# Decode attention with two layers of cached K and V: packets of wo, the place where p is turned, and the size of the chain's bursts

## The chip, the cores and the metric

The kernel runs on one core of one Trainium2 chip. The metric is the device time of one execution in microseconds. Ten runs of the kernel before have a median of 1128.28 us (1122.96 to 1136.9).

## What is computed

Eight batch elements, one token each (D = 448), pass twice through the same two blocks. Block A is attention over a cache: 16 query heads of 256, 8 K/V heads, 4096 cached positions. Block B is a small mixer and MLP. With one token the mixer's shifted parts are all zero, so that `hs` is zero and `x1 = x`. The core of the reference:

```python
def A(x, k_cache, v_cache, wq, wo):          # k_cache, v_cache: (8, 8, 4096, 256)
    q = (x @ wq).reshape(B, 1, 16, 256).transpose(0, 2, 1, 3)
    k, v = repeat(k_cache, 2, axis=1), repeat(v_cache, 2, axis=1)
    p = softmax(einsum("bhqd,bhkd->bhqk", q, k) * 256 ** -0.5)
    o = einsum("bhqk,bhkd->bhqd", p, v)
    return o.transpose(0, 2, 1, 3).reshape(B, 1, 4096) @ wo

x = x + A(layernorm(x), k_cache, v_cache, wq, wo)
x = x + B(layernorm(x), w1, w2, w3, w4)      # ends in x1 + gelu(layernorm(x1) @ w3) @ w4
x = x + A(layernorm(x), k_cache, v_cache, wq, wo)
x = x + B(layernorm(x), w1, w2, w3, w4)
```

K and V of one element and one pass are 32 MB in bfloat16. Both passes read the same caches, and the second pass of an element can start only when the first has gone through the whole of both blocks.

## The kernel before

**Slots and items.** SBUF has 15 slots of 1 MB, [128, 4096] bfloat16. A task is (pass, element, pair of K/V heads). It has 8 items: four slots of K and four of V. `items` (lines 534 to 542) holds their order, in which the K items of one task alternate with the V items of the task before: K, V, K, V. Each item works on one slot, then the slot's place goes back to `places` (line 804), and `emit_loads` (line 559) issues the next load into it from SyncE (line 576). The order of the loads is that of the items.

**What stays.** Of each element, the eleven slots in `kept` (line 63) stay in SBUF from pass 0 to pass 1, and a twelfth is held in four PSUM banks (`away`, line 609, and `back`, line 616). While the eleven are held, four slots are left to circulate.

**A K item.** `transpose_k` (line 579): two VectorE transposes of 32x32 blocks in place (L584, 1219 ns each). Then `step`, then `scores` (line 586): 32 products (L592) in two halves of 16; the second half reads what the second transpose wrote. After the second and the fourth K item of a task, `exps` (line 600) lets ScalarE write p. After the first K item of the next task, `transpose_p` (line 623) turns p with four products against an identity (L628), and ScalarE copies the result into `ptw` (L635). Kept K's are not transposed again in pass 1.

**A V item.** `step`, then `pv` (line 640): 16 products of `ptw` with the slot (L647). In the last eight V items of the program `pv_cols` (line 656) takes the slot as weights instead (L661), in columns of d.

**The chain of an element.** When half of an element's head pairs are done in pass 0, `first_half` (line 452) is added, and when all are, `chain` (line 461): the sums of exp (`z_cols`, line 395), the turn of o to columns (`half`, line 426, L443), products with wo (`add_cols`, line 328, L339), the norm (line 198), w3 (`mlp_hidden`, line 350, L357), w4 (`out_cols`, line 321, L339), and the projection of q for pass 1 (`project_q`, line 277, L285). They are generators. Each `yield` ends a burst. `first_last`, `last` and `rest` are the same for pass 1; `rest` does blocks A's end and B for the first four elements together.

**The order.** It is written out in the program's own order on every engine. `step(idx)` (line 696) is called twice per item, before its products (lines 743, 761) and at its end (line 806). It lets each kind of generator go to its next `yield` when it is behind its pace:

```python
if e["n"] < e["of"] * (idx - e["at"] + 1) / max(e["until"] - e["at"], 1):
```

`of` is the number of bursts that `add_gen` is told, `at` and `until` the items between which they are to be spread. So at most two bursts of a kind fall on one item. `spread_q` (line 297, L305 and L311) places the new q for the scores before the first K item of a new element and pass; a chain that is not through by then is run to its end there (lines 726 and 727).

**Where d lies.** `half` turns o in two products (line 443), of d 0 to 127 and of d 128 to 255, so `OT[:, j, h]` holds d = 128 j + partition of head h. wo is loaded with row g x 128 + partition in `wo_sb[partition, g]` (line 678), and `OT[:, i % 2, i // 2]` is multiplied with `wo_sb[:, i]`.

Of the kernel before, what the change touches and what calls it, by code (L numbers as in the profile page):

```python
# [17 lines left out]
def kernel(  # L18
# [27 lines left out]
    nc = tc.nc  # L46
# [3 lines left out]
    Dh = A_k_cache.shape[3]  # L50
# [6 lines left out]
    NB2 = HD // 128  # L57
    HC = F // 128
# [218 lines left out]
    def project_q(b0, nb, qT):  # L277

        yield from norm(xT[:, :, b0 : b0 + nb], nb, False)
        q_ps = room_ps("q", nb).rearrange("p (c b) -> p c b", b=nb)  # L280
        for j in range(2):
            for h in range(Hq):
                for fc in range(4):
                    w, xi = wblk(wq_sb, HD, 2 * h + j, fc)
                    nc.tensor.matmul(  # L285
                        q_ps[:, j * Hq + h, :],
                        w,
                        xbs(nb)[:, xi, :],
                        start=(fc == 0),
                        stop=(fc == 3),  # L290
                    )
                if h % 8 == 7:
                    yield
        nc.vector.tensor_copy(qT, q_ps)
        yield
# [21 lines left out]
    def y_room(nb):  # L317

        return room_ps("y", nb).rearrange("p (u f b) -> p u f b", u=2, b=nb)

    def out_cols(rhs, w, n, b0, nb, every):

        y_ps = y_room(nb)[:, 0]
        yield from add_cols(y_ps, rhs, w, range(n), every)
        xs = xT[:, :, b0 : b0 + nb]
        nc.vector.tensor_add(xs, xs, y_ps)
# [23 lines left out]
    def mlp_hidden(b0, nb):  # L350

        yield from norm(xT[:, :, b0 : b0 + nb], nb, True)
        h_ps = room_ps("h", nb)
        for c in range(HC):
            for fc in range(4):
                w, xi = wblk(w3_sb, F, c, fc)
                nc.tensor.matmul(  # L357
                    h_ps[:, c * nb : c * nb + nb],
                    w,
                    xbs(nb)[:, xi, :],  # L360
                    start=(fc == 0),
                    stop=(fc == 3),
                )
            if c == HC // 2:
                yield
        yield
        g_t = chn.tile([128, 2, HC * MID], FP32, tag="g")
        hh, g0 = g_t[:, 0, 0 : HC * nb], g_t[:, 1, 0 : HC * nb]
        if nb == 1:
            HT_t = chn.tile([128, HC, 1], BF16, tag="HT")  # L370
            HT = HT_t[:]
        else:
            HT = HTw[:, :, b0 : b0 + nb]

        nc.vector.tensor_scalar_mul(hh, h_ps, 0.5)  # L375
        nc.vector.scalar_tensor_tensor(g0, hh, 2 * 0.044715, h_ps, ALU.mult, ALU.mult)
        nc.vector.scalar_tensor_tensor(g0, g0, 1.0, h_ps, ALU.add, ALU.mult)
        nc.scalar.activation(g0, g0, ACT.Tanh, scale=0.7978845608028654)  # L378
        yield
        nc.vector.scalar_tensor_tensor(  # L380
            HT,
            g0.rearrange("p (c b) -> p c b", b=nb),
            1.0,
            hh.rearrange("p (c b) -> p c b", b=nb),
            ALU.add,
            ALU.mult,
        )
        yield
        return HT

    def mlp(b0, nb):
        HT = yield from mlp_hidden(b0, nb)
        yield from out_cols(lambda c: HT[:, c, :], w4_sb, HC, b0, nb, 2)

    def z_cols(zall, gps):

# [29 lines left out]
    def half(o_ps, zall, g8, OT):  # L426


        rz = yield from z_cols(zall, range(2 * g8, 2 * g8 + 2))

        R = chn.tile([128, 8], FP32, tag="R")
        nc.vector.tensor_mul(
            R[:].rearrange("p (g n) -> p g n", n=4),
            rz[:].rearrange("p n g -> p g n"),
            fold[:].rearrange("p (g n) -> p g n", n=4),
        )
        o_sb = chn.tile([128, Dh], FP32, tag="o_sb")
        nc.scalar.copy(o_sb[:], o_ps[:, 0:Dh])  # L438
        in_use.remove(o_ps)
        yield  # L440
        ot_ps = ot_bank[:, 32 * g8 : 32 * g8 + 16].rearrange("p (j h) -> p j h", j=2)
        for j in range(2):
            nc.tensor.matmul(  # L443
                ot_ps[:, j], o_sb[:, 128 * j : 128 * j + 128], R[:], start=True, stop=True
            )
        yield
        nc.vector.tensor_copy(OT[:, :, 8 * g8 : 8 * g8 + 8], ot_ps)
        yield
# [3 lines left out]
    def first_half(b, st):  # L452

        OT = work.tile([128, 2, Hq, 1], BF16, tag="OT", bufs=1)
        st["OT"] = OT
        yield from half(st["o", 0], st["z"], 0, OT[:, :, :, 0])
        yield from add_cols(
            y_room(1)[:, 0], lambda i: OT[:, i % 2, i // 2], wo_sb, range(NB2 // 2), 2
        )

    def chain(b, st):
        OT = st["OT"]
        yield from half(st["o", 1], st["z"], 1, OT[:, :, :, 0])
        yield from add_cols(
            y_room(1)[:, 1], lambda i: OT[:, i % 2, i // 2], wo_sb, range(NB2 // 2, NB2), 2
        )
        xs = xT[:, :, b : b + 1]
        nc.vector.tensor_add(xs, xs, y_room(1)[:, 0])
        nc.vector.tensor_add(xs, xs, y_room(1)[:, 1])
        yield from mlp(b, 1)  # L470
        qT = chn.tile([128, NB2], BF16, tag="qT2", bufs=2)
        yield from project_q(b, 1, qT[:].unsqueeze(2))
        state[1, b] = {"qT": qT}
# [21 lines left out]
    def rest():  # L495

        yield from out_cols(lambda i: OT2[:, i % 2, i // 2, :MID], wo_sb, NB2, 0, MID, 1)
        yield from mlp(0, MID)
        nc.vector.memset(HTw[:, :, 0:MID], 0.0)
        yield  # L500
# [82 lines left out]
            w = t[:].bitcast(U32).rearrange("p (y e w) -> p y e w", e=2, w=64)[:, :, half]  # L583
            nc.vector.transpose(w, w)  # L584

    def scores(t, x, qbd, gp):
        kv = t[:].rearrange("p (k t e i r) -> p k e r t i", k=4, t=4, e=4, r=2)
        for n in range(8):
            half, e2, par = n // 4, (n // 2) % 2, n % 2
            ep = 4 * e2 + 2 * par + half  # L590
            for k in range(4):
                nc.tensor.matmul(  # L592
                    sc[32 * k : 32 * k + 8, 128 * x : 128 * x + 128],
                    qbd[:, ep, gp].rearrange("p a h -> p (a h)"),
                    kv[:, k, 2 * half + e2, par],
                    start=(n == 0),
                    stop=(n == 7),
                )
# [57 lines left out]
    def pv_cols(o_ps, v, a, gp):  # L656

        g = 2 * gp + a // 2
        for y in range(16):
            for j in range(2):  # L660
                nc.tensor.matmul(  # L661
                    o_ps[:, j, 2 * g : 2 * g + 2],
                    v[:, y * Dh + 128 * j : y * Dh + 128 * j + 128],
                    ptw[:, a, 4 * (y % 4) + y // 4, 6:8],
                    start=(a % 2 == 0 and y == 0 and j == 0),
                    stop=(a % 2 == 1 and y == 15),
                    skip_group_check=True,
                )
# [6 lines left out]
    ps0 = rows_to_cols(x_row, Bn)  # L675
    nc.vector.tensor_copy(xT[:], ps0)
    emit_loads(5)
    nc.sync.dma_start(wo_sb[:], A_wo.rearrange("(g p) d -> p g d", p=128))
    load_split(w3_sb, B_w3, F)
    nc.sync.dma_start(w4_sb[:], B_w4.rearrange("(c p) d -> p c d", p=128))  # L680
    for _ in project_q(0, Bn, qT1[:]):
# [11 lines left out]
    def add_gen(kind, b, g, at, until, total):  # L693
        gens.append({"kind": kind, "b": b, "g": g, "at": at, "until": until, "n": 0, "of": total})

    def step(idx):

        for kind in ("chain", "last", "rest"):
# [5 lines left out]
            if e["n"] < e["of"] * (idx - e["at"] + 1) / max(e["until"] - e["at"], 1):  # L704
                e["n"] += 1
                if next(e["g"], gens) is gens:
                    gens.remove(e)

    first_of = {}
    for idx, (n, kv, c) in enumerate(items):  # L710
        first_of.setdefault((tasks[n][:2], kv), idx)
# [2 lines left out]
    for idx, it in enumerate(items):  # L714
        n, kv, c = it
        ps, b, gp = tasks[n]
        if (ps, b, gp, kv, c) == (0, Bn - 1, REST, 0, 0):
            assert pairs_done[1, MID - 1] == 4
            add_gen("rest", 0, rest(), idx + 1, idx + 18, 21)
        p = where[(b, gp), (kv, c)] if ps == 1 and (stays(it) or inside(it)) else where[it]  # L720
        slot = slots[p]
        final = (ps, b) == (1, Bn - 1)
        if kv == 0:
# [17 lines left out]
            if not (ps == 1 and stays(it)):  # L741
                transpose_k(slot)
            step(idx)
            scores(slot, c, st["q"], gp)
            if c == 0 and n - 1 in p_of:
                transpose_p(p_of.pop(n - 1))
            if c == 1:
                p_n = work.tile([128, 4, 32, 4], BF16, tag="p_sb", bufs=1)
                p_of[n] = p_n
# [5 lines left out]
        else:  # L755
# [34 lines left out]
            if c == 3:  # L790
                done = pairs_done[ps, b] = pairs_done.get((ps, b), 0) + 1
                if done == 2 and ps == 0:
                    add_gen("chain", b, first_half(b, st), idx + 1, idx + 21, 9)
                elif done == 2:
                    add_gen("chain" if final else "last", b, first_last(b, st), idx + 1, idx + 13, 9)
                elif done == 4 and ps == 0:
                    add_gen("chain", b, chain(b, st), idx + 1, first_of[(1, b), 0] - 1, 30)
                elif done == 4 and not final:
                    add_gen("last", b, last(b, st), idx + 1, idx + (7 if b == Bn - 2 else 13), 6)
        if not (ps == 0 and stays(it)):  # L800
# [78 lines left out]
```

The softmax here doesn't subtract the row's maximum and nothing guards it: scores larger than these inputs give would overflow.

## Time and profile before

| | |
|---|---|
| Median of ten runs | 1128.28 us |
| Profiled execution | 1129.44 us, its span 1127.6 us |
| TensorE matmul busy | 713.9 us, 63% of the span |
| TensorE weight load busy | 523.8 us, 46% |
| VectorE busy | 590.9 us, 52% |
| ScalarE busy | 124.3 us, 11% |
| GpSimd busy | 15.7 us, 1% |
| Mean granted TensorE clock | 0.611 |
| Read from HBM | 446.77 MB, 396 GB/s over the span |
| Loads of 1 MB slots | 416 (200 K, 216 V), on SyncE's queue |
| Load of wo | one, 3584 KB, issued at 11.42 us |

How to read what follows. The page of a profile has the busy time of each engine, and the span cut into 40 slices of 28.19 us; for each slice it gives the busy share in tenths, and for the DMA engines the GB/s that they moved. In a timeline a line has the start in us, the time that a group of like instructions took, engine and line of the code, operation, what it writes and reads with the shapes, and the number of instructions; in brackets stands the idle time of the engine before it and what ended it. PE is TensorE's products, PEld its weight loads, DVE is VectorE, ACT ScalarE, SPq SyncE's queue of DMA issues. In a list of waits a line has who waited for whom: us in total, times, longest. Matmuls are pipelined and their ends are modelled, so the busy time of TensorE says less than when a group begins.

### The profile page before, as it was taken

How to read it: one execution, taken by the hardware profiler on the slowest of the kernel's cores; microseconds unless marked ns; L12 is line 12 of the kernel's file. 1: busy time of each engine (PE TensorE's matmuls, PEld its weight loads, DVE VectorE, ACT ScalarE, POOL GpSimd, SP SyncE). 2: the span in 40 equal slices, each digit the busy share in tenths (PEclk: the TensorE clock that was granted, in tenths of full speed). 3: DMA queues.
4: the chain of work that ended last, by engine and by line, in shares of the span. 5: the costliest groups of instructions: out<-in, count | busy, mean ns of one | idle time of the engine just before them, and what ended most of it. 6: DMA issues, size and time to landing. Idle time of an engine off the chain costs nothing. (4 is left out here: it accounts for less than half of the span.)

```text
span 1127.6 us, 36977 instructions
## 1 busy us (share of the span) xinstructions
PE 713.9 (63%) x17173; PEld 523.8 (46%) x17173; DVE 590.9 (52%) x1009; ACT 124.3 (11%) x362; POOL 15.7 (1%) x25
## 2 busy tenths in 40 slices
PE   3145677656864577546785477845777476867676
PEld 2123455434642455424564255623565355655555
DVE  5145454646365555546366463655537553575462
ACT  0001001110110011100011001101011001111010
POOL 0000000000000000000000000000000000000000
PEclk9999999655565555655555555555555555565565
DMA  9999999999999999999999999999999999999994
GB/s 353 371 420 420 413 376 408 418 416 391 402 419 421 386 390 417 418 421 391 374 421 419 420 392 400 421 419 417 403 401 419 416 397 392 419 370 398 391 418 177
DMA packets 67242, 449.15 MB, mean 398 GB/s; under 512 B 6921, under 2 KB 12945, under 8 KB 13457
## 3 DMA queue, kind: packets, MB, share of 16 engines
q1 hardware_dynamic: 67056, 446.80, 97.9%
q8 instruction: 134, 2.20, 0.8%
q14 instruction: 20, 0.16, 0.0%
q10 hardware_dynamic: 32, 0.00, 0.0%
HBM read 446.77 MB, written 0.01 MB: 396 GB/s over the span
## 5 line engine op out<-in xcount | busy, mean ns | idle before, releaser
L584 DVE STREAM_TRANSPOSE slot<-slot 128x1024 uint32<-128x1024 uint32 x400 | 469.5, 1219 | 270.8 <-DMA slot<-in_A_k_cache_dram 263.9
L592 PE MATMUL sc<-slot,qbd 128*8 128x128 bf16 x8192 | 280.6, 295 | 291.9 <-DVE slot L584 239.4
L592 PEld LDWEIGHTS <-qbd 128*8 128x8 bf16 x8192 | 198.4, 109 | 369.8 <-issue 189.1
L647 PE MATMUL o<-slot,ptw 128*8 128x256 bf16 x3968 | 250.5, 400 | 60.4 <-DMA slot<-in_A_v_cache_dram 40.6
L601 ACT ACTIVATE p_n<-sc 128x256 bf16<-128x256 f32 x128 | 95.7, 748 | 767.4 <-PE sc L592 767.4
L647 PEld LDWEIGHTS <-ptw 128*8 128x8 bf16 x3968 | 111.8, 112 | 108.0 <-issue 55.8
L339 PEld LDWEIGHTS <-wo_sb 128*128 128x128 bf16 (+1 forms) x1600 | 63.6, 123 | 21.4 <-issue 21.0
L339 PE MATMUL misc<-OT,wo_sb 128*128 128x1 bf16 (+1 forms) x1280 | 54.3, 176 | 7.2 <-issue 5.0
L285 PEld LDWEIGHTS <-wq_sb 128*128 128x128 bf16 x1152 | 34.9, 104 | 25.2 <-issue 19.5
L311 DVE TENSOR_SCALAR qbd<-misc,quad 128x64 bf16<-128x64 f32 x64 | 13.8, 278 | 60.0 <-PE misc L305 60.0
L635 ACT CAST ptw<-misc 128x128 bf16<-128x128 f32 x64 | 17.4, 272 | 201.6 <-PE misc L628 111.1
L285 PE MATMUL misc<-xb,wq_sb 128*128 128x1 bf16 x1024 | 32.3, 165 | 8.6 <-DVE xb L260 4.4
L601 ACT ACTIVATION_READ_ACCUMULATOR p_n<-sc 128x1 f32 x128 | 33.9, 265 | 0.0
L443 PEld LDWEIGHTS misc<-R,o_sb 128*128 128x128 f32 x124 | 28.0, 314 | 10.4 <-issue 8.2
L443 PE MATMUL misc<-R,o_sb 128*128 128x8 f32 x124 | 30.8, 359 | 1.1 <-ACT o_sb L438 1.1
L243 POOL TENSOR_TENSOR t<-t,nhalf 128x2 f32<-128x2 f32 (+2 forms) x18 | 13.3, 740 | 1098.3 <-DVE t L250 1098.3
L339 PEld LDWEIGHTS <-w_sb 128*128 128x128 bf16 (+1 forms) x630 | 25.0, 125 | 6.0 <-issue 5.8
L357 PE MATMUL misc<-xb,w_sb 128*128 128x1 bf16 (+1 forms) x560 | 17.9, 165 | 12.4 <-DVE xb L260 7.4
L357 PEld LDWEIGHTS <-w_sb 128*128 128x128 bf16 x560 | 17.7, 105 | 17.0 <-issue 16.9
L412 PE MATMUL misc<-zm,one 128*128 128x8 f32 (+1 forms) x66 | 18.8, 355 | 9.4 <-ACT ptw L635 6.5
L619 DVE STREAM_TRANSPOSE slot<-store 128x512 uint32<-128x512 uint32 x32 | 20.1, 685 | 7.2 <-PE sc L592 7.2
L415 DVE RECIPROCAL rz<-misc 128x8 f32<-128x8 f32 (+1 forms) x33 | 6.3, 192 | 32.4 <-PE misc L412 30.6
(94 smaller groups left out, 256.6 us busy)
## 6 DMA issues: line engine op xcount, KB each, us to landing
slot<-in_A_v_cache_dram SPq DMA_DIRECT2D x216, 1024.0 KB, 11.6
slot<-in_A_k_cache_dram SPq DMA_DIRECT2D x200, 1024.0 KB, 12.3
wo_sb<-in_A_wo_dram SPq DMA_DIRECT2D x1, 3584.0 KB, 26.7
wq_sb<-in_A_wq_dram SPq DMA_DIRECT2D x3, 1024.0 KB, 6.9
w_sb<-in_B_w_dram SPq DMA_DIRECT2D x1, 1568.0 KB, 12.7
w_sb<-in_B_w_dram SPq DMA_DIRECT2D x3, 448.0 KB, 26.6
wq_sb<-in_A_wq_dram SPq DMA_DIRECT2D x2, 256.0 KB, 10.1
w_sb<-in_B_w_dram SPq DMA_DIRECT2D x2, 112.0 KB
```

The source lines that it names most:

```text
L285: nc.tensor.matmul(q_ps[:, j * Hq + h, :], w, xbs(nb)[:, xi, :], start=(fc == 0), stop=(fc == 3),)
L311: nc.vector.tensor_scalar_mul(qbd[:, :, :, a, :], qs.rearrange("p e (f g u h) -> p (e f) u g h", f=2, u=2, h=2)[:, :, u], quad[:, a : a + 1],)
L339: nc.tensor.matmul(r, w[:, i, lo:hi], rhs(i), start=start, stop=stop, skip_group_check=open is not None,)
L357: nc.tensor.matmul(h_ps[:, c * nb : c * nb + nb], w, xbs(nb)[:, xi, :], start=(fc == 0), stop=(fc == 3),)
L412: nc.tensor.matmul(z_ps, ones, zm[:], start=True, stop=True)
L443: nc.tensor.matmul(ot_ps[:, j], o_sb[:, 128 * j : 128 * j + 128], R[:], start=True, stop=True)
L584: nc.vector.transpose(w, w)
L592: nc.tensor.matmul(sc[32 * k : 32 * k + 8, 128 * x : 128 * x + 128], qbd[:, ep, gp].rearrange("p a h -> p (a h)"), kv[:, k, 2 * half + e2, ...
L601: nc.scalar.activation(p_sb[:, :, :, 2 * u : 2 * u + 2].rearrange("p t i x -> p x t i"), sc[:, 256 * u : 256 * u + 256].rearrange("p (x t ...
L619: nc.vector.transpose(slot[:].bitcast(U32)[:, 512 * n : 512 * n + 512], store[n][:].bitcast(U32))
L635: nc.scalar.copy(ptw[:, :, :, 6:8], pt_ps.rearrange("p t k (a h) -> p a (t k) h", a=4),)
L647: nc.tensor.matmul(o_ps[32 * q : 32 * q + 8, 0:256], ptz[:, at : at + 8], v[:, y * Dh : (y + 1) * Dh], start=(begin and y < 4), stop=(y >= ...
```

## The change

Three edits, and what follows from them.

1. **wo.** Row (h x 256 + 2 x partition + j) of wo now goes to `wo_sb[partition, 2 h + j]`. Two neighbouring rows of 896 bytes go to one partition, as one run of 1792 bytes. So that OT fits, `half` takes every second column of `o_sb` as weights, and `pv_cols` every second column of the V slot: `OT[:, j, h]` holds d = 2 x partition + j.
2. **p.** `transpose_p` is called inside `scores` of the first K item of the next task, between the 16th and the 17th product, instead of after the 32nd.
3. **Bursts.** `project_q` yields after every 4 heads (16 products) instead of 8, `mlp_hidden` after every 4 columns blocks (16 products) instead of twice in all, and the products with wo in pass 0 and with w4 after every block of columns (16 and 14) instead of every two. The numbers of bursts told to `add_gen` are raised to match: 9 to 11, 30 to 40, 21 to 25.

The products, their number, the transposes and the loads of K and V are the same, and so is the order of the loads on SyncE's queue.

```diff
@@ project_q
-                if h % 8 == 7:
+                if h % 4 == 3:
                     yield
@@ mlp_hidden
-            if c == HC // 2:
+            if c % 4 == 3:
                 yield
@@ mlp
-        yield from out_cols(lambda c: HT[:, c, :], w4_sb, HC, b0, nb, 2)
+        yield from out_cols(lambda c: HT[:, c, :], w4_sb, HC, b0, nb, 1)
@@ half
-                ot_ps[:, j], o_sb[:, 128 * j : 128 * j + 128], R[:], start=True, stop=True
+                ot_ps[:, j], o_sb[:].rearrange("p (i j) -> p j i", j=2)[:, j], R[:], start=True, stop=True
@@ first_half
-            y_room(1)[:, 0], lambda i: OT[:, i % 2, i // 2], wo_sb, range(NB2 // 2), 2
+            y_room(1)[:, 0], lambda i: OT[:, i % 2, i // 2], wo_sb, range(NB2 // 2), 1
@@ chain
-            y_room(1)[:, 1], lambda i: OT[:, i % 2, i // 2], wo_sb, range(NB2 // 2, NB2), 2
+            y_room(1)[:, 1], lambda i: OT[:, i % 2, i // 2], wo_sb, range(NB2 // 2, NB2), 1
@@ scores
-    def scores(t, x, qbd, gp):
+    def scores(t, x, qbd, gp, between=None):
         kv = t[:].rearrange("p (k t e i r) -> p k e r t i", k=4, t=4, e=4, r=2)
         for n in range(8):
             half, e2, par = n // 4, (n // 2) % 2, n % 2
+            if n == 4 and between is not None:
+                between()
@@ pv_cols
-                    v[:, y * Dh + 128 * j : y * Dh + 128 * j + 128],
+                    v[:, y * Dh + j : (y + 1) * Dh : 2],
@@ the loads at the start
-    nc.sync.dma_start(wo_sb[:], A_wo.rearrange("(g p) d -> p g d", p=128))
+    nc.sync.dma_start(
+        wo_sb[:].rearrange("p (h j) d -> p h (j d)", j=2),
+        A_wo.rearrange("(h p j) d -> p h (j d)", p=128, j=2),
+    )
@@ the loop over the items
+    def TURN(n):
+        return 0
...
-            add_gen("rest", 0, rest(), idx + 1, idx + 18, 21)
+            add_gen("rest", 0, rest(), idx + 1, idx + 18, 25)
...
-            scores(slot, c, st["q"], gp)
-            if c == 0 and n - 1 in p_of:
-                transpose_p(p_of.pop(n - 1))
+            turn = None
+            if c == TURN(n) and n - 1 in p_of:
+                turn = lambda t=p_of.pop(n - 1): transpose_p(t)
+            scores(slot, c, st["q"], gp, between=turn)
...
-                    add_gen("chain", b, first_half(b, st), idx + 1, idx + 21, 9)
+                    add_gen("chain", b, first_half(b, st), idx + 1, idx + 21, 11)
...
-                    add_gen("chain", b, chain(b, st), idx + 1, first_of[(1, b), 0] - 1, 30)
+                    add_gen("chain", b, chain(b, st), idx + 1, first_of[(1, b), 0] - 1, 40)
```

## The prediction

> **What bounds the kernel now.** I read the page's slices and queues first: how full are the DMA engines, and where not?
>
> ```profile
> DMA  9999999999999999999999999999999999999994
> GB/s 353 371 420 420 413 376 408 418 416 391 402 419 421 386 390 417 418 421 391 374 421 419 420 392 400 421 419 417 403 401 419 416 397 392 419 370 398 391 418 177
> q1 hardware_dynamic: 67056, 446.80, 97.9%
> ```
>
> The DMA engines are busy all the time, but the busy share hides the loss; the GB/s line shows it. Undisturbed slices move 421 GB/s, so one 1 MB slot takes 1.0486/421 = 2.49 us. Adding (421 - r)/421 x 28.19 us over slices 3 to 39 gives 36.4 us lost, 32.3 of it in the sixteen slices at 403 or below. Those come in eight groups, one for each batch element.
>
> Next, what the load queue waits for: SyncE's own waits.
>
> ```profile
> SPq L576 <- PE o L647: 204.7, 134, 7.3
> SPq L576 <- DVE slot L584: 184.2, 63, 5.0
> SPq L576 <- PE sc L592: 105.7, 117, 3.3
> ```
>
> A load is issued when PV (L647) or scores (L592) has read its slot. Where eight loads are queued this costs nothing. The stretches (view by windows: PE, PEld, DVE, ACT, POOL busy with counts, clock, DMA share, GB/s) tell full from thin:
>
> ```profile
> 38.00:46.00 8.00, 0.00 (x0) 0.00 (x0) 0.00 (x0) 0.00 (x0) 0.00 (x0) 1.00 1.09 333
> 60.00:100.00 40.00, 17.86 (x402) 10.84 (x405) 21.86 (x24) 3.80 (x11) 0.00 (x0) 1.00 1.01 420
> 374.00:430.00 56.00, 39.09 (x898) 28.84 (x901) 28.03 (x68) 5.25 (x16) 1.25 (x2) 0.50 0.98 387
> ```
>
> The first is the load of wo, the second ordinary work, the third a thin stretch: eleven slots hold what pass 1 will reuse, four slots circulate (K, V, K, V), and the chain of one batch element runs on TensorE at half clock. In its timeline a K slot goes: issued 381.17, transposes 387.90 to 390.27, scores done and reissued 391.00: 9.83 us, against 4 x 2.49 = 9.96 us for four slots at full rate. K has no slack. A V slot needs about 6.7 + 1.0 us, so some 2 us of slack, and between a K's scores and the V's products lie chain work and the turning of p:
>
> ```profile
> 380.53 0.60 PE L592 MATMUL sc<-slot,qbd 128*8 128x128 bf16 x16 [0.53 <-DVE zs_t L401]
> 381.06 0.29 PE L628 MATMUL misc<-identb,p_n 128*128 128x32 bf16 x4
> 381.17 0.33 SPq L576 DMA_DIRECT2D slot<-in_A_k_cache_dram  x1
> 381.43 0.27 ACT L635 CAST ptw<-misc 128x128 bf16<-128x128 f32 x1 [4.47 <-PE misc L628]
> 381.75 0.59 PE L412 MATMUL misc<-zm,one 128*128 128x8 f32 x2 [0.41 <-ACT ptw L635]
> 382.28 1.02 PE L647 MATMUL o<-slot,ptw 128*8 128x256 bf16 x16
> 383.35 0.33 SPq L576 DMA_DIRECT2D slot<-in_A_v_cache_dram  x1
> ```
>
> See two things: TensorE idles 0.53 us between two halves of a scores group, waiting for the second transpose; then it turns p, idles 0.41 us for ScalarE's copy, and only then frees the V. A long burst:
>
> ```profile
> 406.97 0.60 PE L592 MATMUL sc<-slot,qbd 128*8 128x128 bf16 x16 [0.53 <-DVE slot L584]
> 407.50 1.93 PE L339 MATMUL misc<-HT_t,w_sb 128*128 128x1 bf16 x42
> 407.61 0.33 SPq L576 DMA_DIRECT2D slot<-in_A_k_cache_dram  x1
> 409.36 1.03 PE L647 MATMUL o<-slot,ptw 128*8 128x256 bf16 x16
> 410.43 0.33 SPq L576 DMA_DIRECT2D slot<-in_A_v_cache_dram  x1
> ```
>
> Here 42 w4 products hold the V back 1.8 us; the two issues lie 2.82 us apart, over the 2.49 of a slot.
>
> **What the Trainium skill says.** "DMA: Bandwidth & Descriptors", section "Why small descriptors are slow", puts a fixed cost on each packet. The trace agrees: its packet records have a median of 46 ns for 896 bytes and 309 ns for 8192, a line with about 14 ns fixed. The same page, "Anatomy of one DMA", says that most of a fixed 2 us is the receipt after the last byte (of GpSimd's path; these loads are SyncE's). Here the packets of a load ended at 385.89 and its transposes began at 387.90: 2.0 us. "TensorE: Matmul & The Clock Gate", section on weight-path modes, says the fast weight load applies to 128 non-FP32 columns, "packed or strided"; "SBUF — State Buffer", "Door 1", lets up to 8 bf16 of stride read free. No strided 128-column bf16 load exists before, so no row tests these two.
>
> **The change, part by part.**
>
> wo. 4096 packets of 896 bytes become 2048 of 1792. Now 3.67 MB at 333 GB/s take 11.0 us. Per packet and engine that is 43 ns, against 311 ns for 8192 bytes at 421 GB/s; the line between gives 76 ns at 1792, so 2048 x 76/16 = 9.7 us. I take 1.2 us gained, behind a full queue, so at the end too. Bounds: 2.3 us gained if packets cost nothing (3.67/421 = 8.7); 1.7 lost if they run as the 1792-byte packets of the w3 halves (median 99.5 ns, 12.7 us).
>
> Turning p. The four products (0.29 us) now stand after 16 of 32 scores. For a K that is transposed they fall into the 0.53 us hole, cost nothing, and ScalarE's copy runs beside the second half. The V after it is freed 0.29 + 0.41 = 0.7 us sooner, about 0.6 where L412 follows. If the hole is absent because TensorE is late, 0.29 us goes onto a K slot: at two turns in each of eight thin stretches, 4.6 us at worst. Kept K's have no hole, but free no load there that is late.
>
> Bursts. The products are the same; the instruction order of both kernels shows them moved. Between K and V: w3 32 to 16 (0.5 us less; its 1.0 us wait for xb, through VectorE and GpSimd, stays), w4 42 to 28 (1.0 less, since the slow 64-column ones move behind the V), 8 w3 products new after a turn (0.25 more), 16 wo products new in a place that had none. There the V was issued 0.85 us after the K; 1.4 is still under 2.49, so nothing. VectorE's and ScalarE's small steps and GpSimd's power move with them by an item or two; what is queued behind them on VectorE is the next K's transposes, mostly waiting for their load anyway. At a chain's end, two bursts of 32 wq products now stand between V's; the load behind had about 2.7 us to spare: nothing (at most 0.5 each if not). In the first chain 48 wq products now precede the spreading of q; scores of pass 1 come 2 us later, with 2.3 us of queued transfers as cover: nothing, 2 us if gone. No DMA moves to another queue; SyncE's order stays.
>
> What late V's cost now, from the packet records: the time between the ends of successive loads above 2.49 us, for loads whose slot such a V freed, all eight stretches, capped by what the V gains: turn with L412 1.9; w3 burst 1.9; w4 burst 1.1; turn alone 0.8; first chain (bursts of 56 and 64, two turns) 1.6; one V at 989.3 behind a turn and 56 products 0.6. Sum 7.9 us. What is late next is K: 9.83 against 9.96 leaves nothing to make up, so a gap closed partly reopens one load later. I take half, 3.9 us; bounds 0 and 7.9 plus a fifth of the 21 us lost at K loads, 12.
>
> Strided weights. L443 (fp32) and L661: nothing; bound in the second rival.
>
> Sum: 1.2 + 3.9 = 5.1 us. The profiled execution took 1129.44 us (span 1127.6, 1.84 around it) and would take 1124.3; it lies 1.2 above the median of ten, 1128.28, so the median becomes 1123.2.
>
> **Rivals.** (1) K sets the pace: V's slack was cover already, only wo counts. For it: 9.83 us. Against: V loads lose about 24 us, as much as K loads. 1128.3 - 1.2 = 1127.1, up to 1131 if turns land on late K's. (2) Slower: strided weight loads at L661 run without the fast path. The price is in this trace:
>
> ```profile
> 1107.59 0.93 PEld L661 LDWEIGHTS <-slot 128*128 128x128 bf16 x32
> 1108.97 0.93 PEld L339 LDWEIGHTS <-wo_sb 128*64 128x64 bf16 x16
> ```
>
> 32 full loads take as long as 16 of 64 columns: 29 ns against 58, so 128 slow columns cost 116, 87 more. Four such groups run at the end with about 1 us idle among them: 128 x 0.087 - 1 = 10.1 us on the closing chain, 1128.3 - 5.1 + 10.1 = 1133.3. It decides from 48 ns more per load, (5.1 + 1)/128; against it is what the skill states. (3) More comes back: evenly spaced V's let the queue refill and K losses fall too: 1.2 + 12 = 13.2 us, 1115.1. For it: losses cluster where one or two loads are in flight.
>
> **Chances.** Forecast 0.45 (own range 1120 to 1126.5), rival 1 0.20, rival 2 0.15, rival 3 0.20. A measurement of this kernel tells about 0.5% (5.6 us) from no change: below 1122.6 is faster, above 1133.9 slower. Faster: 0.20 of the forecast's 0.45 and rival 3's 0.20, 0.40. Slower: 0.07 from rival 2, 0.03 from rival 1 with late turns, 0.10. Same: 0.50. The range 1116 to 1131 leaves out 0.08 of rival 3 and 0.11 of rival 2.
>
> **What would show it.** wo: the window of its load at about 380 GB/s. Turns: PV's waits on ScalarE's copy (16.8 + 11.7 us now) nearly gone, no longer gap in a transposed K. Bursts: V issues in thin stretches within 2.5 us of the K before, those slices up by 5 to 10 GB/s. Wrong if those slices stay as they are though V's come sooner (rival 1), or if 32 weight loads of L661 take over 1.5 us (rival 2).

## The result, and the profile after

The changed kernel takes 1121.68 us (median of 14, 1112.9 to 1128.7) against 1129.57 us for the kernel before, now with 51 runs. The ratio is 0.9922, 95% interval 0.9903 to 0.9942: by the ratio 8.8 us faster, 6.5 to 11.0 (the two medians differ by 7.9). A second set of runs gave 0.9906 (0.9883 to 0.9928). The forecast was 5.1 us faster and 1123.2 us; the time lies in the range, and the sign is right. The size is not: the gain is larger than forecast, and nearly all of it comes with one part of the change.

The profiled execution took 1125.93 us (span 1124.1). It is one of the slower of its kernel, so its losses are a little above the typical ones. Its slices and queue, then SyncE's waits:

```profile
DMA  9999999999999999999999999999999999999994
GB/s 354 383 420 420 408 367 408 420 408 387 414 419 419 398 400 420 418 420 398 417 420 419 420 402 404 418 420 402 379 417 418 407 383 412 419 362 411 396 412 165
q1 hardware_dynamic: 65008, 446.80, 97.9%
```

```profile
SPq L576 <- DVE slot L584: 221.2, 77, 4.5
SPq L576 <- PE o L649: 205.6, 142, 7.3
SPq L576 <- PE sc L594: 150.4, 157, 5.1
```

The busy digits and the 97.9% are those of before. The GB/s line is not: by the same sum over slices 3 to 39, 33.0 us are lost instead of 36.4, and the second slice, which holds the small packets, rose from 371 to 383. The three longest of SyncE's waits add up to more than before (577 us against 495), but the whole list doesn't: 931 us against 941. The waits went to other names, so this list doesn't tell better from worse.

The stretches by windows (columns as before), with the one that holds the load of wo:

```profile
27.00:35.00 8.00, 2.61 (x68) 1.75 (x68) 3.71 (x4) 1.01 (x3) 0.00 (x0) 1.00 1.06 381
60.00:100.00 40.00, 17.70 (x396) 10.86 (x388) 21.72 (x24) 3.77 (x11) 0.00 (x0) 1.00 1.01 420
374.00:430.00 56.00, 40.66 (x919) 29.33 (x910) 27.61 (x68) 5.25 (x16) 1.25 (x2) 0.50 1.00 399
```

One reading of the prediction has to be put right here. It showed the stretch 38 to 46 us as the load of wo. That stretch holds mostly the load of w4 (896-byte packets too). The load of wo runs from about 25 us on; in the kernel before, its own stretch reads:

```profile
27.00:35.00 8.00, 2.61 (x68) 1.77 (x68) 3.40 (x4) 1.01 (x3) 0.00 (x0) 1.00 1.09 340
```

340 against 381 GB/s for 3.67 MB is 10.8 against 9.6 us: 1.2 us.

The thin stretch moves 399 instead of 387 GB/s. One window of one profile doesn't show that the change did this: p_wo (below), which leaves the order of the work in that stretch as it was, has nearly the same there.

```profile
374.00:430.00 56.00, 39.35 (x896) 29.24 (x900) 28.16 (x68) 5.21 (x16) 1.25 (x2) 0.50 0.99 397
```

The turn of p, in the timeline of the changed kernel:

```profile
379.22 0.29 PE L630 MATMUL misc<-identb,p_n 128*128 128x32 bf16 x4
379.58 0.27 ACT L637 CAST ptw<-misc 128x128 bf16<-128x128 f32 x1 [3.35 <-PE misc L630]
379.81 0.60 PE L594 MATMUL sc<-slot,qbd 128*8 128x128 bf16 x16 [0.31 <-DVE zs_t L401]
380.34 0.60 PE L412 MATMUL misc<-zm,one 128*128 128x8 f32 x2
380.45 0.33 SPq L576 DMA_DIRECT2D slot<-in_A_k_cache_dram  x1
380.87 1.02 PE L649 MATMUL o<-slot,ptw 128*8 128x256 bf16 x16
381.94 0.33 SPq L576 DMA_DIRECT2D slot<-in_A_v_cache_dram  x1
```

The turn lies in the hole between the halves, ScalarE's copy is over (379.85) when the second half has hardly begun (379.81), and V follows K by 1.49 us instead of 2.18. The w4 burst of the same element:

```profile
406.17 0.60 PE L594 MATMUL sc<-slot,qbd 128*8 128x128 bf16 x16 [0.53 <-DVE slot L584]
406.70 0.90 PE L339 MATMUL misc<-HT_t,w_sb 128*128 128x1 bf16 x28
406.81 0.33 SPq L576 DMA_DIRECT2D slot<-in_A_k_cache_dram  x1
407.54 1.03 PE L649 MATMUL o<-slot,ptw 128*8 128x256 bf16 x16
408.49 1.47 PE L339 MATMUL misc<-HT_t,w_sb 128*64 128x1 bf16 x28
408.61 0.33 SPq L576 DMA_DIRECT2D slot<-in_A_v_cache_dram  x1
```

28 products stand ahead of the V and the 28 slow ones behind it: the two issues are 1.8 us apart, not 2.82. At the end of the program:

```profile
1104.21 0.93 PEld L663 LDWEIGHTS <-slot 128*128 128x128 bf16 x32
1105.59 0.93 PEld L339 LDWEIGHTS <-wo_sb 128*64 128x64 bf16 x16
```

32 strided weight loads take 0.93 us, as the contiguous ones did. Rival 2 is ruled out.

### The profile page after: what moved, and what is told of

Same layout as the page of the kernel before. It is cut to its first block, busy times and chain, and to the rows that moved or that the text cites. A ratio compares the mean times of both kernels' runs of the same rounds, so it can differ in the third digit from the quotient of the medians.

```text
span 1124.1 us, 36998 instructions
## 1 busy us (share of the span) xinstructions
PE 717.4 (64%) x17173; PEld 520.0 (46%) x17173; DVE 591.2 (53%) x1009; ACT 124.6 (11%) x362; POOL 15.7 (1%) x25
## 3 DMA queue, kind: packets, MB, share of 16 engines
q1 hardware_dynamic: 65008, 446.80, 97.9%
## 5 line engine op out<-in xcount | busy, mean ns | idle before, releaser
L594 PE MATMUL sc<-slot,qbd 128*8 128x128 bf16 x8192 | 285.5, 292 | 316.0 <-DVE slot L584 250.2
L594 PEld LDWEIGHTS <-qbd 128*8 128x8 bf16 x8192 | 192.0, 107 | 386.9 <-issue 208.6
L339 PEld LDWEIGHTS <-wo_sb 128*128 128x128 bf16 (+1 forms) x1600 | 65.0, 123 | 24.7 <-issue 24.1
L339 PE MATMUL misc<-OT,wo_sb 128*128 128x1 bf16 (+1 forms) x1280 | 57.7, 176 | 1.7 <-issue 1.7
L285 PEld LDWEIGHTS <-wq_sb 128*128 128x128 bf16 x1152 | 34.7, 104 | 24.4 <-issue 18.6
L443 PEld LDWEIGHTS misc<-R,o_sb 128*128 128x128 f32 x124 | 28.0, 312 | 9.9 <-issue 7.8
L443 PE MATMUL misc<-R,o_sb 128*128 128x8 f32 x124 | 30.9, 360 | 0.0
L357 PEld LDWEIGHTS <-w_sb 128*128 128x128 bf16 x560 | 18.3, 105 | 18.1 <-issue 18.1
L339 PE MATMUL misc<-HT_t,w_sb 128*128 128x1 bf16 (+1 forms) x560 | 23.4, 177 | 1.7 <-DVE HT_t L380 1.7
```

The source lines that it names most:

```text
L285: nc.tensor.matmul(q_ps[:, j * Hq + h, :], w, xbs(nb)[:, xi, :], start=(fc == 0), stop=(fc == 3),)
L339: nc.tensor.matmul(r, w[:, i, lo:hi], rhs(i), start=start, stop=stop, skip_group_check=open is not None,)
L357: nc.tensor.matmul(h_ps[:, c * nb : c * nb + nb], w, xbs(nb)[:, xi, :], start=(fc == 0), stop=(fc == 3),)
L443: nc.tensor.matmul(ot_ps[:, j], o_sb[:].rearrange("p (i j) -> p j i", j=2)[:, j], R[:], start=True, stop=True)
L594: nc.tensor.matmul(sc[32 * k : 32 * k + 8, 128 * x : 128 * x + 128], qbd[:, ep, gp].rearrange("p a h -> p (a h)"), kv[:, k, 2 * half + e2, ...
```

## The experiments

**Theories.** Late V's (the prediction's): a V whose products start more than about 1.5 us after its K's scores (2.49 less the 1.03 of its products) leaves the DMA engines short; K has no slack. Rivals: K alone sets the pace; only the largest burst counts, wherever it lies; or TensorE's time counts in any place.

All ratios are to the kernel before, five rounds each, on one chip for each set of four.

| Kernel | Ratio, 95% interval | Late K | Late V | Lost at K, us | Lost at V, us |
|---|---|---|---|---|---|
| before | 1 | 0 of 71 | 28 of 87 | 24.0 | 21.2 |
| p_wo | 0.9982, 0.9967 to 0.9998 | 2 of 73 | 32 of 90 | 25.3 | 18.7 |
| p_turn | 0.9996, 0.9979 to 1.0014 | 2 of 74 | 33 of 92 | 23.8 | 22.1 |
| p_bursts | 0.9929, 0.9904 to 0.9953 | 1 of 74 | 17 of 97 | 24.7 | 16.2 |
| p_turn_bursts | 0.9908, 0.9884 to 0.9932 | 0 of 75 | 16 of 94 | 20.9 | 14.5 |
| after_again | 0.9906, 0.9883 to 0.9928 | 0 of 75 | 17 of 95 | 19.8 | 15.0 |
| l_late | 1.0046, 1.0027 to 1.0065 | 27 of 75 | 3 of 79 | 30.2 | 19.3 |
| l_early | 1.0166, 1.0133 to 1.0199 | 0 of 72 | 52 of 87 | 29.6 | 36.2 |
| b_late | 1.0053, 1.0034 to 1.0071 | 21 of 73 | 12 of 82 | 28.1 | 20.7 |
| p_late | 0.9993, 0.9976 to 1.0009 | 23 of 74 | 10 of 85 | 26.2 | 20.8 |
| skip | 0.9886, 0.9855 to 0.9917 | 1 of 71 | 12 of 88 | 19.0 | 12.1 |
| d_v | 1.0469, 1.0446 to 1.0492 | 9 of 70 | 60 of 100 | 33.7 | 55.1 |
| d_k | 1.0282, 1.0257 to 1.0307 | 17 of 84 | 19 of 110 | 38.1 | 39.8 |

The two columns of late items are counted in the one profile of each kernel, between 75 and 1060 us, over items whose slot was reissued while at most two earlier loads still ran. A K is late when its scores end over 0.9 us after its transposes (0.65 is the rule). A V is late when its products start over 1.5 us after the item before.

The last two columns come from the DMA packets of the same profiles: the time between the ends of successive loads above 2.49 us, summed over the loads from the 17th on, by the kind of item that had freed the slot. The first profile of the changed kernel has 24.4 and 18.5. Single profiles scatter: before, p_wo and p_turn, whose bursts are the same, differ by 1.5 us at K's and 3.4 at V's.

A late item isn't by itself a lost load. In the kernel before, the loads into slots of the 28 late V's took 0.25 us longer than 2.49 on average, those into slots of the 59 timely ones 0.19; only in l_early is the difference large (0.53 against 0.08). In l_late the loads behind late K's lost 0.25, those behind timely ones 0.34. So the counts tell where the work stands, and the sums what it costs.

**Each part alone.** p_wo:

```diff
-    nc.sync.dma_start(wo_sb[:], A_wo.rearrange("(g p) d -> p g d", p=128))
+    nc.sync.dma_start(
+        wo_sb[:].rearrange("p (h j) d -> p h (j d)", j=2),
+        A_wo.rearrange("(h p j) d -> p h (j d)", p=128, j=2),
+    )
```

with the two strided weights of the change.

> The kernel before with the new layout of wo alone (its load, and the strided weights of L443 and of the last V items). Theory of the prediction: the load is shorter by 1.2 us behind a full queue and strided weights cost nothing, so 1.2 us faster (ratio 0.999). Rival, strided weights are slow: 32 weight loads of the last V items take well over 1 us and the time rises. Rival, the load is hidden anyway: 0.0.

Measured: 0.9982, 2.0 us faster (0.2 to 3.7). The expected 1.2 lies inside; its profile has 382 GB/s in the window of wo, against 381 in the changed kernel.

p_turn: `transpose_p` between the halves of `scores`, all else as before.

> The kernel before with the turn of p between the halves of scores alone. Theory of late V's: V slots behind a turn are freed 0.6 to 0.7 us sooner; 2 to 3 of the 7.9 us of the sum hang on turns, half of it counted, so 1 to 1.5 us faster (0.999). Rival, K sets the pace: same or up to 4.6 us slower. Rival, most of the change lies here: 5 us faster or more (0.995).

Measured: 0.9996, 0.5 us (2.4 faster to 1.6 slower). The waits went as forecast. Waits on ScalarE's copy in p_turn, the longest of those who wait:

```profile
PE misc L285 <- ACT ptw L637: 3.2, 8, 0.4
DVE OT L447 <- ACT ptw L637: 2.9, 1, 2.9
PEld L649 <- ACT ptw L637: 2.8, 16, 0.3
DVE g_t L375 <- ACT ptw L637: 2.7, 6, 0.8
```

PV's 16.8 + 11.7 us of waiting became 2.8. The time hardly followed, though the interval still holds the expected 1 to 1.5 us. The packet records are clearer: the seven loads behind a turn with L412 lost 1.9 us in the kernel before and 3.3 in p_turn, with their V's 0.7 us sooner. But for two of the 17 (1.34 and 3.15 us), the V's behind a turn had been 0.6 to 1.2 us behind their K, within the 1.5 they may have.

p_bursts: the smaller bursts and the raised numbers of `add_gen`, all else as before.

> The kernel before with the smaller bursts alone. Theory of late V's: about 5 of the 7.9 us hang on bursts, half counted, so 2.5 us faster (0.998); if nothing is lost again, 5 us (0.9955). Rival, K sets the pace: same (1.000).

Measured: 0.9929, 8.0 us faster (5.3 to 10.8): nearly all of the change, more than either number expected for this theory. K's stay on time; V's over 1.5 us fall from 28 to 17, and the time lost at V's from 21.2 to 16.2 us, with 24.0 and 24.7 at K's. The profiled execution was 2.1 us slower than the median of its kernel. The size of the bursts and the raised numbers, which set their pace, were changed together; no run parts them.

p_turn_bursts: both.

> Turn and bursts together, wo as before. If the parts only add: the sum of the two, 4 to 5 us faster (0.996). If the whole change's 0.992 lies in the thin stretches: 7 us faster (0.994). If one part takes away what the other gives: no more than the larger of the two.

Measured: 0.9908, 10.4 us (7.7 to 13.1). That is beyond the plain sum of the expectations, and its interval overlaps that of bursts alone; what the turn adds to small bursts (2.4 us by the medians of the ratios) isn't settled.

**Where the steps stand.** `step` is called in four places: ahead of a K's scores, behind them, ahead of a V's products, behind them. l_late, on the changed kernel:

```diff
             transpose_k(slot)
             step(idx)
+            step(idx)
...
             rz_gp = run(z_cols(st["z"], [gp]))
-            step(idx)
...
         emit_loads()
-        step(idx)
+        if kv == 1:
+            step(idx)
+            step(idx)
```

> The changed kernel with every step of the chain put between a V's products and the next K's scores, none between a K and its V (two steps before a K's scores, two at a V's end). Theory of late V's: V's are freed right behind K's, so faster than the changed kernel by 2 to 4 us (ratio 0.989). Rival, the size of the largest burst is what counts, wherever it lies: bursts here reach 64 products, so near the kernel before (0.998). Rival, K sets the pace: products ahead of K's scores delay K, slower than the changed kernel (0.996 or more).

l_early is its mirror: none ahead of a K's scores, two at a K's end, two ahead of a V's products, none at its end.

> The changed kernel with every step of the chain put between a K's scores and the V's products, none ahead of a K (two steps at a K's end, two before a V's products). Theory of late V's: V's are held back by up to 48 products, slower than the changed kernel by 5 us or more, at or above the kernel before (1.000). Rival, K sets the pace: K's are free of the chain, so faster than the changed kernel (0.989). Rival, only burst size: as the kernel before (0.998).

b_late makes the edit of l_late in the kernel before.

> The kernel before with its large bursts, every step put between a V's products and the next K's scores. Theory of late V's: large bursts do no harm there, so as fast as small bursts alone or faster (0.991). Rivals, burst size, or K sets the pace: bursts of up to 80 products (2.4 us and more) ahead of a K delay it, so no gain or slower (1.000 to 1.005).

Measured: l_late 1.0046, l_early 1.0166, b_late 1.0053. l_early went as late V's expect, and further: 52 of 87 V's are late, no K is. l_late and b_late contradict the theory as I had used it: with hardly a late V left they are slower than the kernel before. About a third of the K's are late now, and the time lost at K's is 30.2 and 28.1 us, against 24.0 in the kernel before. The hole under the transposes is not a free place.

p_late marks each `yield` that a burst or L443 follows, and lets `step` take those only at a V's end or ahead of a K's scores:

```diff
-    def step(idx):
+    def step(idx, tags=(None, "P")):
...
-            if e is None:
+            if e is None or e.get("tag") not in tags:
                 continue
...
-                if next(e["g"], gens) is gens:
+                e["tag"] = next(e["g"], gens)
+                if e["tag"] is gens:
                     gens.remove(e)
...
             transpose_k(slot)
             step(idx)
+            step(idx, ("P",))
...
-            step(idx)
+            step(idx, (None,))
...
         emit_loads()
-        step(idx)
+        if kv == 0:
+            step(idx, (None,))
+        else:
+            step(idx)
+            step(idx, ("P",))
```

> The changed kernel with all bursts of the chain (and L443) kept out of the places between a K and its V, two allowed at a V's end and ahead of a K's scores; the small steps stay in all four places, so that no product waits there for a step of VectorE queued behind a transpose. Theory of late V's: faster than the changed kernel by 2 to 5 us (0.989), and what made all steps behind V slow was the small products. Rival, size of a burst counts in any place (up to 64 here): as all steps behind V, 1.004.

Measured: 0.9993. The whole gain is lost again. Two causes stand in its timeline:

```profile
383.80 0.13 DVE L447 CAST OT<-misc 128x16 bf16<-128x16 f32 x1
383.99 0.56 PE L339 MATMUL misc<-OT,wo_sb 128*128 128x1 bf16 x16 [1.90 <-DVE OT L447]
384.48 1.02 PE L594 MATMUL sc<-slot,qbd 128*8 128x128 bf16 x32
385.55 0.33 SPq L576 DMA_DIRECT2D slot<-in_A_k_cache_dram  x1
386.30 2.62 PE L339 MATMUL misc<-OT,wo_sb 128*128 128x1 bf16 x64
386.45 2.37 DVE L584 STREAM_TRANSPOSE slot<-slot 128x1024 uint32<-128x1024 uint32 x2 [2.51 <-DMA slot<-in_A_k_cache_dram]
388.84 0.39 PE L594 MATMUL sc<-slot,qbd 128*8 128x128 bf16 x8
```

First, 16 products ahead of the K wait 1.90 us for OT, whose copy (L447) is queued on VectorE behind the very transposes of that K; the K's scores start only then. In all, products with wo wait so 8 times, for 16.2 us; in the kernel before none does. My expectation had claimed that no product would wait so. Second, 64 products run as long as the transposes do, so none of the scores runs beside the second transpose. Either way the K is late.

**How much was to be had.** skip leaves out, in pass 0 and for single elements, three of four products for wq and w3 and all but two rows for wo and w4, so the output isn't the reference's; steps and order are those of before.

```diff
-                for fc in range(4):
+                for fc in range(4) if nb > 1 else range(3, 4):
...
```

The same line stands in w3's loop; the rows of wo and w4 are cut in the calls of `add_cols`.

> The kernel before with most of the chain's products left out in pass 0 for single elements: one of four for wq and w3, two of 8 to 16 rows for wo, two of 14 for w4 (its output is not the reference's). The steps and their order stay. What is lost here is not lost to products: if bursts cause the loss that the change removed, at least as fast as the small bursts, 0.990 or lower; most of the 36 us in the thin stretches would stay if the circulation of four slots sets them (0.985), and go if products do (0.970).

Measured: 0.9886, 12.9 us (9.4 to 16.4). So the products left out cost some 13 us in the kernel before, and most of the loss is not theirs: 31.1 us of 45.2 are lost between loads in its profile all the same. Small bursts, with every product in place, gain 8.0; the two intervals overlap.

**The price of TensorE's time in each place.** after_again is the changed kernel once more.

> The changed kernel, as the base for the three runs beside it on the same chip: 0.992 as before. If its wo does nothing beside the other two parts, as turn and bursts without wo (0.991).

d_v and d_k add to it 32 products with an unused result in each of many places:

```diff
+    def extra():
+        if any(e["kind"] == "chain" and e["n"] for e in gens):
+            for _ in range(32):
+                nc.tensor.matmul(
+                    misc[:, 496:497], identb[:], identb[:, 0:1], start=True, stop=True
+                )
```

called ahead of a V's step (d_v) or of the step behind a K's transposes (d_k).

> The changed kernel with 32 extra products of one column (about 1 us at half clock, result unused) ahead of each V item's own steps while a chain is under way, 94 places, some 60 of them in the thin stretches. Theory of late V's: each V is freed 1 us later; some 0.3 us lost at each of the 60, 20 us slower than the changed kernel (1.010). Rival, only K counts: V's slack of 2 us covers it, as the changed kernel (0.992).

> The changed kernel with the same 32 extra products behind the transposes of each K and ahead of its steps, 94 places. Theory of late V's: they lie in the 1.2 us in which TensorE waits for the first transpose, so 0 to 5 us slower than the changed kernel (0.994). Rival, TensorE's time counts wherever it is, or K sets the pace: as much as beside V, 20 us (1.010).

The expected 94 places were a miscount. The traces hold 5056 and 4544 of these products, so 158 places in d_v and 142 in d_k; 42 of the 142 stand ahead of kept K's, which have no transposes.

Measured: medians 1181.82 and 1162.31 against 1118.2, so 63.6 and 44.1 us. With 0.99 us for 32 products (in d_k's timeline) 156 and 141 us of products were added: of the 0.99 us of a place, 0.40 are lost beside a V and 0.31 ahead of a K. Both are far above what was expected, also for so many places (an estimate by the number of places: 34, and 0 to 8), and yet more than half of the added time stays covered in either.

Part of the loss lies in the end: the last element's chain is met too, the time behind the last load grows from 14.7 to 22.6 and 18.9 us, and the losses from the 366th load on by some 15 us in both. Without these two, some 41 and 25 us remain. So a place beside a V costs 1.3 times as much as one ahead of a K, some 1.6 times without the end. The two are no even pair: d_k adds 24.8 us at V's and 18.3 at K's, and l_early loses 29.6 us at K's with no K late, so what stands in one place is paid at loads of both kinds.

## Why the prediction was right, and where not

**wo.** Right, mechanism and size: 1.2 us by the windows, 2.0 (0.2 to 3.7) by p_wo. The line between the two sizes of packet gave 76 ns for 1792 bytes; the median packet now takes 78. Only the stretch shown was that of w4, so 333 stood for 340 GB/s.

**Strided weights.** Right: 32 loads of L663 take 0.93 us, as before. This agrees with the Trainium skill ("TensorE: Matmul & The Clock Gate", the section on weight-path modes), by which the fast weight load reads its columns "packed or strided". The fp32 loads of L443 have a median of 331 ns, 333 before.

**Turning p.** That the turn fits into the hole and the V comes 0.7 us sooner is right. That this gives back the time lost at the loads behind it isn't seen: the term of 1.9 + 0.8 us, half of it counted, stands against 0.5 us (2.4 faster to 1.6 slower), and the loads behind the turns with L412 lose no less. The step that failed counted loss at a load behind a turn as caused by the turn. By the prediction's own slack nearly all of those V's were in time.

**Bursts.** The term was mis-sized the other way. The sum had 1.9 + 1.1 and most of 1.6 + 0.6 for them, some 4.6 us, and "I take half": 2.3. Measured 8.0 (5.3 to 10.8). The step that failed is the halving, which rested on "a gap closed partly reopens one load later". In p_bursts the time lost at V's fell by 5.0 us, and that at K's stayed (24.0 and 24.7): nothing of the kind reopened. At V's all four profiles with small bursts lose less (14.5 to 18.5 us) than the three with large ones (18.7 to 22.1). Rival 3 had it that K losses fall too; at K's the four have 24.7, 20.9, 24.4 and 19.8, so that is not settled. Its number, 13.2 us, lies outside the interval of the whole change. Why bursts give more than the 4.6 us stays open.

How the lost time is divided depends on the way of counting: the prediction had about 24 us at V's and 21 at K's, the columns of the table have 21.2 and 24.0 for the same profile.

**The sum.** Without the halving it would be 7.9 + 1.2 = 9.1 us, close to the 8.8. That would be luck: the turn was put too high and the bursts too low.

**Products moved behind a V "cost nothing".** True as the change does it (no K of 75 is late), false as a rule: l_late, p_late and d_k show the limit. K's lack of slack, which the prediction read from 9.83 against 9.96 us, fits this; no run varies it.

**Rivals.** "K sets the pace" fails as the sole cause: p_bursts gains 8 us with K as it was. That only the largest burst counts fails too: l_late and l_early both hold large blocks (up to 64 and 48 products), the one with the larger is the faster, and they differ by 1.2%. That TensorE's time counts in any place is nearer to the truth than expected, as d_v and d_k both cost; but the change leaves TensorE's work as it was and gains all the same, so the place counts too. What fits these runs is two places with limited cover, each charged for what exceeds it; smaller bursts split the same work between both. That is an account that fits, not one that was tested load by load.

Open is what the turn and wo add on top of small bursts: the intervals of 0.9929, 0.9908, 0.9906 and 0.9922 overlap.

## What to carry to other kernels

Where a few buffers circulate between DMA and two kinds of consumers, read how long each buffer's round is against the time of all transfers in it: here that told which consumer had room, but not how much a place would cost. Put side work into every place in portions below the cover of that place, rather than all of it into the place that looks idle. A wait that disappears from the list can be worth nothing if the waiter was within its slack. Read differences of single profiles against kernels that leave the place in question alone.

## What was not expected of the hardware

DMA engines that were busy all the time in a window (1.00 and 1.01 in the two stretches of the changed kernel above) moved 399 in one and 420 GB/s in the other, of the same 8192-byte packets: the share of busy time didn't tell a thin queue from a full one. The number of loads under way did. In the kernel before, a load that was issued while one other still ran ended 2.97 us after the load ahead of it on average, with two others 2.65, with three to seven 2.51 to 2.53. This doesn't part a queue that is too short from a load that was issued too late.
